# A convolution and gated MLP on one core: the steady step as one flat list, instruction by instruction

## The chip, the core and the metric

The kernel runs on one core of one Trainium2 chip. The metric is device time in microseconds for one execution. Before the change three executions gave 2262.18 to 2262.81 us, median 2262.51. Engine names are those of the profile: PE (TensorE matmul), PEld (its weight loads), DVE (VectorE), ACT (ScalarE), POOL (GpSimd), SP (SyncE, which here only issues DMAs).

## The reference

All data is fp32. `x` is 8 × 4096 × 192; a causal convolution of 7 taps with weights per head, then an MLP of width 2048 with the quick gelu:

```python
w = exp(weight - max(weight)); w = w / (sum(w) + 1e-9)          # (8 heads, 7 taps)
x_pad = concatenate([zeros(B, 6, D), x], axis=1)
c = einsum('hk,bskhg->bshg', w, x_pad[:, idx, :])               # causal, 7 taps, each head its weights
h = c.reshape(32768, 192) @ w_in                                # (192, 2048)
g = h * (1.0 / (1.0 + exp(-1.702 * h)))
out = g @ w_out                                                 # (2048, 192)
```

## The kernel before

The 32768 tokens go through in 32 steps (`big`), each 2 × 512 tokens, and every step has two matrix products. Both are done by bilinear forms in the manner of Strassen: some products of blocks are saved, at the price of sums of blocks before and after.

**First product** (`product1`, L598), `x` by `w_in`. A step has two halves (`v`) of 20 terms, listed in `TERMS`; each term is two calls, one per row group of the PE array (partitions 0 to 63 and 64 to 127, tiles of 64 × 128, 512 columns). That is 80 calls. They write PSUM tiles of two banks (`slots`, `sums`; a tile is a name like "a4" while it is in use), which are then combined: DVE sums (`sum2`, L639), ACT copies, also with changed sign (`copy2`, L633 and L635) and the gelus on ACT (`gelu`, L615 from PSUM, L620 from SBUF), which write the blocks of `g`. A call of an fp32 matmul is two weight loads and two passes in the profile.

**Second product** (`second`, L837; `one_matmul`, L855), `g` by `w_out`. It uses tiles of 128 × 32 and 256 columns, so four column strips of PE can run side by side: three main strips (the three chunks of one form) and one side strip, which works through other forms chunk by chunk. `go` (L871) issues three main calls and one side call, 78 times: 312 calls. When a chunk of the side strip is done, an ACT copy takes it to SBUF (L880), written directly behind that call. The main strips go to `mains = (bs[0], bx[0], by[0])`, the side strip to `sides = (bx[1], bs[1], by[1])`, the six banks of the three PSUM tiles that are free at that point. Around it stand DVE sums of blocks of `g` (`sum_g`, L355 and L357), accumulating transfers issued by POOL (`acc`, L831), seeds and joins of partial results (ACT L884, DVE), the 32 × 32 turns of the result on DVE (L771) and the stores on SP (L782).

**Convolution of later steps.** In between, the next steps' inputs are made: loads of `x` (`load_x`, L78, SP), transposes (L438, DVE), taps on ACT (`tap`, L483), their sums by POOL additions (`next_add`, L501) or accumulating transfers (`add_taps`, L506, POOL), sums of the blocks (`sums_c`, on POOL) and transfers to the other half of the partitions (`cross`, L526, SP).

**What sets the order.** The program has a manual schedule: each engine executes its instructions in the order in which they are written, and semaphores join the engines. The steady step is written by two lists, `ORDER` for the first product and `PLAN` for the second, and by queues of pending work beside them (`todo`, `ready`, `adds`, `tree`, `pieces`, `sums_left`): an entry like `("tap",)` or `("add", 4)` takes the next item or items of a queue, and `need`, `end_taps` and the loops at the end of `second` empty what is left. A term, a sum or a copy of `ORDER` is always written for both banks at once, and `("go", n)` always writes three main calls and one side call. The opening has a list of its own (`OPENING`).

Of the kernel before, what the change touches and what calls it, by code (L numbers as in the profile page):

```python
# [10 lines left out]
AF = mybir.ActivationFunctionType  # L11
# [4 lines left out]
def kernel(  # L16
# [149 lines left out]
    def side(big, other, b):  # L166
        return cross_of(big, b) if other else slot_of(big, b)
# [20 lines left out]
    def form(i):  # L188
# [8 lines left out]
    COPY_O = [  # L197
        [(10, 2), (16, 1), (17, 0), (18, 0), (8, 7), (9, 5), (11, 3, -1), (12, 6, -1)],
        [(13, 3), (14, 3), (15, 0), (19, 4), (20, 4), (21, 5), (22, 7)],
        [],  # L200
        [(23, 1), (24, 1), (1, 14), (7, 0, -1)],
    ]
    SUMS_O = [
# [4 lines left out]
    ]  # L208
    TURN_O = (9, 17, 20, 21)

# [105 lines left out]
    def split_rest(i, part=slice(0, PIECE)):  # L316

        lo, hi, m, e = words(i, part)
        ef = e.bitcast(F32)
        act.activation(ef, e, AF.Relu, bias=bias[:, 0:1], scale=-1.0)  # L320
        act.activation(e, ef, AF.Relu, bias=bias[:, 1:2], scale=-(2.0**23))
# [43 lines left out]
    w_left = list(SUMS_W)  # L365

    def next_w(n):
        for _ in range(n):
            add_up(lambda j: w_in_s[:, j, :], *w_left.pop(0))

# [6 lines left out]
    def round_o(i):  # L377
# [15 lines left out]
        round_piece(NW + i, dsts)  # L393

    def add_forms(stage):
        for dst, src, *sign in COPY_O[stage]:
            if sign:
                act.mul(form(dst), form(src), -1.0)
            else:
                act.copy(form(dst), form(src))  # L400
        for dst, src in SUMS_O[stage]:
            nc.gpsimd.dma_start(out=form(dst), in_=form(src), accum_op=ALU.add)

    def end_forms():
        for i in TURN_O:
            act.mul(form(i), form(i), -1.0)
# [45 lines left out]
    def tap_home(big, c, k):  # L452
        if big == 1:
# [8 lines left out]
    def conv(big, c, k, ns=slice(0, 2), times=vec.tensor_scalar_mul):  # L462
        src = conv_src(big, c, k, ns)
        dst = own(big)[:, 2 * c + ns.start : 2 * c + ns.stop, :]
        tap = cw[:, c, k : k + 1]
        if k == 0:
            times(dst, src, tap)
# [5 lines left out]
    DMA_TAPS = (0,)  # L473
    TAPS_IN = (0, 2, 1)
    ADDS_IN = [(1, 6), (2, 5), (2, 6)] + [(c, k) for c in (2, 1) for k in range(1, K) if (c, k) not in ((1, 6), (2, 5), (2, 6))]
    TREE = {2: [(1, 2)], 4: [(3, 4)], 6: [(5, 6), (0, 1), (3, 5), (0, 3)]}
    TREE_1 = {2: {2: [(1, 2)], 4: [(3, 4), (0, 1)], 6: [(5, 6), (0, 3), (0, 5)]}, 0: {2: [(1, 2)], 4: [(3, 4)], 6: [(5, 6)]}}

    def tap(big, c, k):

        dst = own(big)[:, 2 * c : 2 * c + 2, :]
        home = tap_home(big, c, k) if k else dst
        act.mul(home, conv_src(big, c, k), cw[:, c, k : k + 1])  # L483
        if k and c not in DMA_TAPS and big > 1:
            adds.append((ADDS_IN.index((c, k)), dst, home))
            adds.sort(key=lambda a: a[0])
            if big == 2:
                next_add()
            return
        homes = [dst] + [tap_home(big, c, i) for i in range(1, K)]  # L490
        for a, b in (TREE if big > 1 else TREE_1[c]).get(k, ()):
            tree.append((homes[a], homes[b]))
        if big < 3:
            end_taps(2 if big == 2 and k == K - 1 else 0)

    tree, adds = [], []

    def next_add():
        if adds:
            _, dst, home = adds.pop(0)  # L500
            nc.gpsimd.tensor_add(dst, dst, home)  # L501

    def add_taps():
        if tree:
            out, src = tree.pop(0)
            nc.gpsimd.dma_start(out=out, in_=src, accum_op=ALU.add)  # L506

    def add_pair(c, a, b):

        dst = own(1)[:, 2 * c : 2 * c + 2, :]  # L510
        homes = [dst] + [tap_home(1, c, i) for i in range(1, K)]
        vec.tensor_add(homes[a], homes[a], homes[b])

    def end_taps(left=0):
        while len(tree) > left:
            add_taps()
# [13 lines left out]
    def copy_over(b):  # L530

        for o in range(2):
            act.copy(conv_t[halves[1 - o], cross_of(0, b), :], own(0)[halves[o], b, :])

    pieces, sums_left = [], []
    LAST_AT = {s[0]: i for i, s in enumerate(SUMS_C)}
    ENDS = (NBLK, NBLK + 3, NBLK + 6, NB - 2, NB)
    GROUPS = [range(*ends) for ends in zip(ENDS, ENDS[1:])]  # L540

    def cross_piece():
        if pieces:
            cross(*pieces.pop(0))

    def cross_blocks(big):

        bs = list(REST)
        while bs:
            n = 1  # L550
            while n < min(3, len(bs)) and bs[n] == bs[0] + n:
                n += 1
            pieces.append((big, bs[0], bs[0] + n))
            bs = bs[n:]

    def next_sum():
        if sums_left:
            big, i = sums_left.pop(0)
            sums_c(big, *SUMS_C[i])
            for b in GROUPS:  # L560
                if max(LAST_AT[s] for s in b) == i:
                    pieces.append((big, b[0], b[-1] + 1))

    def begin_sums(big):
        sums_left.extend((big, i) for i in range(len(SUMS_C)))

    def prepare(big):

        for k in range(K if big < 3 else 0):
            yield "", 0.76 if k else 0.48, lambda k=k: conv(big, 1, k)  # L570
        yield f"conv {big}", 0.0, lambda: None
        def done():
            need(f"taps {big}")
            while adds:
                next_add()
            if OPEN_SUM:
                sums_c(big, *OPEN_SUM)
            cross(big, OPEN, OPEN + 1)

        yield f"done {big}", 0.0, done  # L580

    def prepare_taps(big):

        order = [(c, k) for c in (0, 2) for k in range(K)]
        if big > 2:
            order = [(c, 0) for c in TAPS_IN] + [(c, k) for c in TAPS_IN for k in range(1, K)]
        for c, k in order:
            yield "", 1.0, lambda c=c, k=k: tap(big, c, k)
        yield f"taps {big}", 0.0, lambda: None

    def product1(slot, a, b, big, v, first=False):
# [3 lines left out]
        for h in range(2):  # L595
# [11 lines left out]
    ALL = slice(0, TOK)  # L607

    def gelu(b, u, v, src, sign=1):
# [3 lines left out]
        if isinstance(src, list):  # L613
            for h in range(2):
                act.activation(  # L615
                    dst[:, :, h, :], src[h].rearrange("p (o t) -> p o t", o=2), AF.Gelu_apprx_sigmoid,
                    scale=float(sign),
                )
        else:
            act.activation(  # L620
                dst.rearrange("p o h t -> p h o t"),
                src.rearrange("p h (o t) -> p h o t", o=2),
                AF.Gelu_apprx_sigmoid,
                scale=float(sign),
            )
# [3 lines left out]

    def copy2(dst, src, sign=1):  # L630
        for h in range(2):
            if sign == 1:
                act.copy(bank(dst, h), bank(src, h))  # L633
            else:
                act.mul(bank(dst, h), bank(src, h), -1.0)  # L635

    def sum2(op, dst, a, b):
        for h in range(2):
            op(*(bank(t, h) for t in (dst, a, b)))  # L639

    def plain(u, m, n, v, slot, ks=range(NC), first=0):

        for k in ks:
            product1(slot, NC * (2 * u + m) + k, 2 * k + n, 0, v, k == first)

    ORDER = [
        (0, "prod", 6, "a8"), (0, "sum", "k0", "a8", "-", "k8"), (0, "prod", 2, "a3"), (0, "copy", "k4", "a3", 1),
        (0, "prod", 12, "a2"), ("tap",), ("tap",), ("tap",), ("tap",), ("add", 4), (0, "prod", 16, "a0"),
# [615 lines left out]
```

## Time and profile before

| what | us |
|---|---|
| median of three executions | 2262.51 |
| profiled execution: time | 2262.78 |
| profiled execution: span | 2261.1 |
| PE busy in the span | 2248.2 |
| DVE busy | 1985.3 |
| ACT busy | 1707.7 |
| POOL busy | 1063.9 |
| a steady step, first product and second | 35.42 and 33.95 |
| start of the second product of step 1 | 136.80 |

The page gives busy times over the whole span, the chain of work that ended last, and groups of instructions by line. PE's passes overlap, so it counts as busy while it waits for a fraction of a microsecond; where it waits is read from the starts of its weight loads and passes in the timeline. Row times are from the span's start. In a row of the timeline, the bracket gives the idle time before it and what ended it.

### The profile page before, as it was taken

The numbers are of one execution on the slowest core, as the hardware profiler recorded it, in microseconds if no ns is written. First come the engines' busy times: TensorE is split into PE (matmuls) and PEld (weight loads), VectorE is DVE, ScalarE is ACT, GpSimd is POOL, SyncE is SP. The second block draws the span as 40 slices with busy tenths as digits, with TensorE's granted clock in tenths as the row PEclk, the third lists the DMA queues.
The fourth block names the chain that finished last, engine by engine and source line by source line (L and its number), as shares of the span: only waits on it lengthen the run. The fifth ranks groups of instructions, "written<-read, shape, count | busy, mean of one in ns | idle before, by whom it ended". The sixth has DMA issues, their size and how long they took to land.

```text
span 2261.1 us, 62136 instructions
## 1 busy us (share of the span) xinstructions
PE 2248.2 (99%) x24966; PEld 1552.0 (69%) x24966; DVE 1985.3 (88%) x2970; ACT 1707.7 (76%) x3233; POOL 1063.9 (47%) x1098
## 2 busy tenths in 40 slices
PE   9999999999999999999999999999999999999999
PEld 5366567766777766777667776667776677766775
DVE  8998888988889888889888898888988888988888
ACT  8677877777777778777787777787777877777754
POOL 1545544455543555444555445554355544455510
PEclk9999999999999999999999999999999999999999
DMA  8986657766667666576565776666866657765543
GB/s 198 174 158 133 125 114 150 143 128 127 121 131 159 128 128 126 111 160 140 125 132 114 141 152 128 129 124 118 163 134 128 124 114 151 144 127 103 104 92 71
DMA packets 275679, 298.05 MB, mean 132 GB/s; under 512 B 119104, under 2 KB 203328, under 8 KB 275392
## 3 DMA queue, kind: packets, MB, share of 16 engines
q0 software_dynamic: 57648, 150.69, 37.0%
q1 hardware_dynamic: 216096, 142.99, 27.8%
q8 instruction: 198, 3.24, 0.6%
q14 instruction: 89, 0.73, 0.1%
q10 hardware_dynamic: 1648, 0.39, 0.1%
HBM read 53.15 MB, written 25.17 MB: 35 GB/s over the span
## 4 chain that ended last, share of the span: by engine, by line
PE 96%; DVE 2%; ACT 1%; issue 1%; DMA 1%; POOL 0%; DVEq 0%; ACTq 0%; POOLq 0%; SPq 0%
PE slot L598 49%; PE slot L855 45%; PE slot L1120 1%; DVE g L357 1%; DMA g<-osbs 0%; PE slot L1115 0%; DVE room L357 0%; ACT g L615 0%; PE slot L946 0%; DVE room L639 0%; ACT w_form L483 0%; DMA xin<-in_x_dram 0%; DVE slot L639 0%; DVE room L355 0%; DVE osbs L771 0%
## 5 line engine op out<-in xcount | busy, mean ns | idle before, releaser
L598 PE MATMUL slot<-conv_t,w_in_s 64*128 64x512 f32 x5152 | 1147.4, 594 | 3.3 <-ACT room L633 1.5
L598 PEld LDWEIGHTS slot<-conv_t,w_in_s 64*128 64x128 f32 x5152 | 663.3, 186 | 474.6 <-issue 312.1
L855 PE MATMUL slot<-g,w_form 128*32 128x256 f32 x9672 | 894.2, 379 | 0.7 <-DVE room L357 0.7
L855 PEld LDWEIGHTS slot<-g,w_form 128*32 128x32 f32 x9672 | 575.6, 110 | 128.9 <-DVE room L357 2.1
L501 POOL TENSOR_TENSOR conv_t<-conv_t,g 128x512 f32<-128x512 f32 x354 | 449.0, 1275 | 88.4 <-ACT g L483 65.4
L855 PE MATMUL slot<-g,w_out_s 128*32 128x256 f32 x5952 | 467.5, 379 | 1.3 <-DVE g L357 0.8
L357 DVE TENSOR_TENSOR g<-g 128x1024 f32<-128x1024 f32 x372 | 450.4, 1224 | 8.0 <-DMA g<-osbs 1.0
L880 ACT COPY room<-slot 32x256 f32<-32x256 f32 x651 | 237.2, 364 | 289.8 <-PE slot L855 281.5
L639 DVE TENSOR_TENSOR room<-slot,room 128x512 f32<-128x512 f32 x620 | 383.6, 679 | 67.8 <-PE slot L598 67.8
L633 ACT COPY room<-slot 128x512 f32<-128x512 f32 x620 | 337.7, 595 | 77.7 <-PE slot L598 61.7
L483 ACT ACTIVATE g<-xt,cw 128x512 f32<-128x512 f32 x534 | 353.9, 715 | 3.7
L620 ACT ACTIVATE g<-room 128x1024 f32<-128x1024 f32 x248 | 265.7, 1071 | 79.0 <-DVE room L639 49.3
L615 ACT ACTIVATE g<-slot 128x512 f32<-128x512 f32 x528 | 282.5, 610 | 51.9 <-PE slot L598 32.8
L831 POOL DMA_DIRECT2D g<-g x124 | 128.1, 1038 | 355.0 <-PE slot L855 330.8
L639 DVE TENSOR_TENSOR slot<-slot,room 128x512 f32<-128x512 f32 x372 | 239.7, 689 | 53.8 <-PE slot L598 52.2
L855 PEld LDWEIGHTS slot<-g,w_out_s 128*32 128x32 f32 x5952 | 239.7, 110 | 43.2 <-DVE room L639 23.3
L355 POOL TENSOR_TENSOR conv_t<-conv_t 128x256 f32<-128x256 f32 x210 | 179.3, 860 | 129.2 <-PE slot L598 119.6
L855 PE MATMUL slot<-osbs,w_form 128*32 128x256 f32 x2232 | 229.5, 379 | 0.0
L506 POOL DMA_DIRECT2D g<-g x120 | 105.9, 883 | 238.1 <-ACT g L483 99.4
L855 PEld LDWEIGHTS slot<-osbs,w_form 128*32 128x32 f32 x2232 | 132.5, 110 | 23.6
L639 DVE TENSOR_TENSOR slot<-room,slot 128x512 f32<-128x512 f32 x124 | 79.8, 687 | 41.8 <-PE slot L598 41.8
L855 PE MATMUL slot<-room,w_form 128*32 128x256 f32 x1488 | 112.9, 379 | 0.0
(166 smaller groups left out, 1662.6 us busy)
## 6 DMA issues: line engine op xcount, KB each, us to landing
g<-g POOLq DMA_DIRECT2D x124, 512.0 KB, 6.5
xin<-in_x_dram SPq DMA_DIRECT2D x240, 180.0 KB, 4.2
conv_t<-conv_t SPq DMA_DIRECT2D x186, 192.0 KB, 5.4
g<-g POOLq DMA_DIRECT2D x120, 256.0 KB, 5.4
conv_t<-conv_t SPq DMA_DIRECT2D x186, 128.0 KB, 2.9
out_dram<-osbs SPq DMA_DIRECT2D x186, 128.0 KB, 2.7
g<-room POOLq DMA_DIRECT2D x31, 512.0 KB, 5.1
conv_t<-g POOLq DMA_DIRECT2D x60, 256.0 KB, 5.4
```

Source lines behind the costliest of these rows:

```text
L355: eng.tensor_add(v(dst), v(a), v(b))
L357: eng.tensor_sub(v(dst), v(a), v(b))
L483: act.mul(home, conv_src(big, c, k), cw[:, c, k : k + 1])
L501: nc.gpsimd.tensor_add(dst, dst, home)
L598: nc.tensor.matmul(slot[h], w_in_s[halves[h], a, v * P : (v + 1) * P], src, start=first, stop=True, skip_group_check=True,)
L615: act.activation(dst[:, :, h, :], src[h].rearrange("p (o t) -> p o t", o=2), AF.Gelu_apprx_sigmoid, scale=float(sign),)
L620: act.activation(dst.rearrange("p o h t -> p h o t"), src.rearrange("p h (o t) -> p h o t", o=2), AF.Gelu_apprx_sigmoid, scale=float(sign),)
L633: act.copy(bank(dst, h), bank(src, h))
L639: op(*(bank(t, h) for t in (dst, a, b)))
L831: nc.gpsimd.dma_start(out=spot(dst), in_=spot(a), accum_op=ALU.add)
L855: nc.tensor.matmul(dst, w, t, start=first, stop=last, skip_group_check=True)
L880: act.copy(to, d)
```

## The change

`ORDER`, `PLAN` and the queues are gone. One flat list `STEP` has every instruction group of a steady step by itself, and `run(STEP, big)` writes it for steps 2 to 31; `OPENING` likewise has steps 0 and 1. The arithmetic of a step, its 80 and 312 matmul calls and its numbers of sums, copies, gelus and transfers stay. What differs in a steady step:

- Terms, sums, copies and gelus are written per bank (last argument 0 or 1), and the order of terms differs somewhat. Sums and copies of one bank may stand apart from those of the other.
- `("m", i)` is three main calls, `("s", i)` one side call, `("t", i)` the copy of a finished side chunk. Side and main calls are no longer one to one in order: the list begins with `s 0`, `m 0`, `s 4`, `s 5`, `m 2`, `s 2`.
- `sides` is now `(by[1], bx[1], bs[1])`; `mains` is unchanged.
- Of the POOL additions eleven stand in half 0 of the first product and one in half 1. One tap is left in the first product, the others are in the second.
- The loads of `x` come behind the transposes in half 0. Three of the crosses are in the first product, four in the second; all six accumulating transfers of the taps are in the second.

```diff
-    def product1(slot, a, b, big, v, first=False):
+    def product1(slot, a, b, big, v, first=False, hs=range(2)):
...
-        for h in range(2):
+        for h in hs:
...
-        mains, sides = (bs[0], bx[0], by[0]), (bx[1], bs[1], by[1])
+        mains, sides = (bs[0], bx[0], by[0]), (by[1], bx[1], bs[1])
...
+    STEP = [
+        ("prod", 0, 6, "a8", 1), ("prod", 0, 6, "a8", 0), ("sum", 0, "k0", "a8", "-", "k8", 0),
+        ("prod", 0, 12, "a2", 0), ("prod", 0, 2, "a3", 1), ("tap", 1, 1, 6), ("add", 1, 1, 6),
+        ("prod", 0, 12, "a2", 1), ("prod", 0, 2, "a3", 0), ("prod", 0, 16, "a0", 1), ("prod", 0, 16, "a0", 0),
+        ("sum", 0, "k0", "a8", "-", "k8", 1), ("copy", 0, "k4", "a3", 1, 1), ("sum", 0, "a1", "a2", "-", "k0", 0),
+        ("prod", 0, 9, "a2", 0), ("prod", 0, 15, "a3", 1), ("copy", 0, "k4", "a3", 1, 0),
...
+        ("sum", 0, "k5", "a1", "-", "k1", 0), ("prod", 0, 1, "a1", 1), ("sum", 0, "k5", "a1", "-", "k1", 1),
+        ("prod", 0, 10, "a4", 0), ("copy", 0, "a5", "a4", -1, 0), ("prod", 0, 18, "a2", 0), ("prod", 0, 18, "a2", 1),
+        ("add", 1, 1, 4), ("add", 1, 2, 6), ("add", 1, 2, 1), ("xt", 2, 0), ("xt", 2, 2), ("load", 3),
+        ("prod", 0, 10, "a4", 1), ("copy", 0, "a5", "a4", -1, 1), ("prod", 0, 17, "a1", 0), ("prod", 0, 17, "a1", 1),
+        ("copy", 0, "k6", "a2", 1, 1), ("copy", 0, "k6", "a2", 1, 0), ("prod", 0, 19, "a4", 0),
+        ("prod", 0, 19, "a4", 1), ("sum", 0, "a6", "k6", "-", "a4", 0), ("prod", 0, 11, "a1", 0),
+        ("gelu", 0, 0, 1, "a1", 1, 0), ("prod", 0, 11, "a1", 1), ("gelu", 0, 0, 1, "a1", 1, 1),
...
+        ("gelu", 1, 3, 1, "k3", 1, None), ("sum", 1, "k5", "a1", "-", "k1", 0), ("prod", 1, 11, "a1", 0),
+        ("copy", 1, "a5", "a4", -1, 0), ("prod", 1, 19, "a4", 0), ("copy", 1, "a5", "a4", -1, 1),
+        ("prod", 1, 19, "a4", 1), ("copy", 1, "k6", "a2", 1, 0), ("copy", 1, "k6", "a2", 1, 1),
...
+        ("prod", 1, 4, "a6", 1), ("gelu", 1, 0, 0, "a6", 1, 1), ("prod", 2, 0, "a3", 0),
+        ("sum", 1, "k7", "a7", "-", "k6", 1), ("prod", 1, 13, "a4", 1), ("prod", 1, 13, "a4", 0),
+        ("sum", 1, "k9", "a4", "-", "k0", 0), ("vsum", 1, 9), ("sum", 1, "k9", "a4", "-", "k0", 1),
+        ("gelu", 1, 0, 0, "a6", 1, 0), ("begin", 0), ("s", 0), ("final",), ("m", 0), ("s", 4), ("s", 5), ("m", 2),
+        ("s", 2), ("m", 1), ("m", 6), ("m", 5), ("s", 1), ("vsum", 1, 6), ("m", 7), ("m", 4),
+        ("gelu", 1, 2, 0, "k7", 1, None), ("gsum", 14, 14, "-", 18), ("s", 7), ("s", 8), ("m", 3),
...
+        ("tap", 2, 0, 4), ("tree", 2, 0, 3, 4), ("s", 46), ("t", 9), ("m", 50), ("gsum", 20, 20, "-", 11), ("s", 49),
...
+        ("join", "k2", "k2", "-", "k1"), ("turn", 1, 1, 1, "k2"), ("tree", 2, 0, 0, 1), ("turn", 1, 0, 0, "k6"),
+        ("m", 76), ("join", "k1", "p3", "-", "k3"), ("join", "k2", "p2", "-", "k4"), ("end",), ("store", 0, 0),
+        ("turn", 0, 0, 1, "k1"), ("turn", 0, 1, 1, "k2"), ("tree", 2, 0, 3, 5), ("s", 68), ("t", 18), ("m", 77),
+        ("m", 74), ("m", 75), ("join", "k1", "p5", "+", "k5"), ("tap", 2, 2, 6), ("store", 0, 1),
+        ("cross", 1, 12, 14), ("join", "k8", "k8", "+", "k0"), ("turn", 0, 1, 0, "k1"), ("tap", 2, 2, 4),
+        ("turn", 1, 1, 0, "k8"), ("store", 1, 0), ("store", 1, 1), ("tap", 2, 1, 1), ("tree", 2, 0, 0, 3),
     ]
...
+    def main_part(i):
+        dst, w, t, first, last = now["todo"][i]
+        for c in range(NC):
+            one_matmul(chunk(dst, c), w[:, chunk_cols(c)], t, first, last)
+
+    def side_part(i):
+        d, w, t, first, to = now["aside"][i]
+        one_matmul(d, w, t, first, to is not False)
...
+    opening()
+    for big in range(2, N_BIG):
+        run(STEP, big)
```

More of the change, by code (lines that the diff above doesn't have):

```diff
@@ L528, in cross, with copy_over @@
             )
[L530 to L589, printed above, removed]
-    def product1(slot, a, b, big, v, first=False):
+    def copy_over(b, o):
+        act.copy(conv_t[halves[1 - o], cross_of(0, b), :], own(0)[halves[o], b, :])
+    def product1(slot, a, b, big, v, first=False, hs=range(2)):
         s, c = slot_of(big, b), cross_of(big, b)
@@ L1211 @@
[L1211 to L1233 removed]
+            fcopy=form_copy,
```

694 lines of the change are left out of this document (275 added, 419 removed), and 282 rows, old and new, of tables (MAINS, OPENING, ORDER, PLAN).

## The prediction

> **What bounds the kernel now.** First the page: which engine is full, and whose work makes the chain.
>
> ```profile
> span 2261.1 us, 62136 instructions
> PE 2248.2 (99%) x24966; PEld 1552.0 (69%) x24966; DVE 1985.3 (88%) x2970; ACT 1707.7 (76%) x3233; POOL 1063.9 (47%) x1098
> PEclk9999999999999999999999999999999999999999
> PE 96%; DVE 2%; ACT 1%; issue 1%; DMA 1%; POOL 0%; DVEq 0%; ACTq 0%; POOLq 0%; SPq 0%
> ```
>
> PE is full at a full clock, and the chain that ends last is PE for 96%. The change leaves PE's calls as they are (80 and 312 in a step), so only PE's lost time can be won. Next the busy time by windows, one window to a product: two steady steps, then the second product of step 1 and the first of step 2.
>
> ```profile
> 1007.50:1042.92 35.42, 35.42 (x161) 20.68 (x160) 29.86 (x45) 28.71 (x50) 25.02 (x24) 1.00 0.54 112
> 1042.92:1076.87 33.95, 33.95 (x626) 28.69 (x625) 31.02 (x47) 24.82 (x52) 9.40 (x11) 1.00 0.79 154
> 1076.87:1112.28 35.41, 35.41 (x161) 20.67 (x161) 29.85 (x45) 28.68 (x50) 25.02 (x24) 1.00 0.54 113
> 1112.28:1146.22 33.94, 33.94 (x625) 28.81 (x624) 31.02 (x47) 24.80 (x52) 9.40 (x11) 1.00 0.77 152
> ...
> 136.80:172.90 36.10, 34.93 (x625) 22.97 (x625) 33.63 (x46) 24.92 (x52) 11.60 (x14) 1.00 0.79 154
> 172.90:209.09 36.19, 35.94 (x164) 21.98 (x160) 29.79 (x45) 28.71 (x50) 26.61 (x25) 1.00 0.56 119
> ```
>
> The columns are length, then PE, PEld, DVE, ACT, POOL, granted clock, DMA share, GB/s. A steady step is 35.42 + 33.95 = 69.37 us and repeats to 0.02. PE counts as busy throughout, because its passes are pipelined; the lost time shows only in the rhythm of the weight loads. They are in the timeline of the first product (start, length):
>
> ```profile
> 1010.19 0.19 PEld L598 LDWEIGHTS slot<-conv_t,w_in_s 64*128 64x128 f32 x2 [0.24 <-issue]
> 1010.78 6.89 PEld L598 LDWEIGHTS slot<-conv_t,w_in_s 64*128 64x128 f32 x33 [0.40 <-ACT room L633]
> 1017.91 0.52 PEld L598 LDWEIGHTS slot<-conv_t,w_in_s 64*128 64x128 f32 x3 [0.24 <-issue]
> 1018.82 0.29 PEld L598 LDWEIGHTS slot<-conv_t,w_in_s 64*128 64x128 f32 x2 [0.39 <-POOL conv_t L501]
> 1019.29 0.29 PEld L598 LDWEIGHTS slot<-conv_t,w_in_s 64*128 64x128 f32 x3 [0.18 <-ACT slot L635]
> 1019.78 0.23 PEld L598 LDWEIGHTS slot<-conv_t,w_in_s 64*128 64x128 f32 x2 [0.20 <-issue]
> ...
> 1024.08 0.23 PEld L598 LDWEIGHTS slot<-conv_t,w_in_s 64*128 64x128 f32 x2 [0.20 <-issue]
> ...
> 1035.23 0.34 PEld L598 LDWEIGHTS slot<-conv_t,w_in_s 64*128 64x128 f32 x2 [0.17 <-issue]
> 1035.73 0.19 PEld L598 LDWEIGHTS slot<-conv_t,w_in_s 64*128 64x128 f32 x1 [0.16 <-issue]
> 1036.12 0.29 PEld L598 LDWEIGHTS slot<-conv_t,w_in_s 64*128 64x128 f32 x2 [0.20 <-ACT slot L635]
> 1036.62 0.29 PEld L598 LDWEIGHTS slot<-conv_t,w_in_s 64*128 64x128 f32 x3 [0.21 <-ACT slot L635]
> 1037.09 0.26 PEld L598 LDWEIGHTS slot<-conv_t,w_in_s 64*128 64x128 f32 x2 [0.17 <-issue]
> ...
> 1041.87 0.29 PEld L598 LDWEIGHTS slot<-conv_t,w_in_s 64*128 64x128 f32 x2 [0.30 <-DVE slot L639]
> ```
>
> From 1019.78 to 1024.08 ten pairs of loads take 4.30 us: 0.43 us for a pass on each of the two row groups. A product has 160 passes, 80 a group: 34.4 us. So 35.42 holds 1.0 us of loss. Three waits are legible. At 1010.78 a pair comes 0.59 after the last, 0.16 late. From 1017.91 to 1019.78 eight loads (four pairs, 1.72) take 1.87: 0.15. From 1035.23 to 1037.09 again eight take 1.86: 0.14. The rest, 0.55, lies at the ends: the wait of 0.30 at 1041.87, and the turn to the other tile shape.
>
> The second product's rhythm, in PE's timeline:
>
> ```profile
> 1000.57 0.39 PE L855 MATMUL slot<-g,w_out_s 128*32 128x256 f32 x3
> 1000.72 0.38 PE L855 MATMUL slot<-g,w_form 128*32 128x256 f32 x1
> 1000.78 0.39 PE L855 MATMUL slot<-g,w_out_s 128*32 128x256 f32 x3
> ...
> 1007.04 0.39 PE L855 MATMUL slot<-g,w_out_s 128*32 128x256 f32 x3
> ...
> 1041.45 1.54 PE L598 MATMUL slot<-conv_t,w_in_s 64*128 64x512 f32 x4
> 1042.92 0.42 PE L855 MATMUL slot<-g,w_out_s 128*32 128x256 f32 x3
> 1043.11 0.38 PE L855 MATMUL slot<-g,w_form 128*32 128x256 f32 x1
> ```
>
> From 1000.57 to 1007.04 are 30 rounds, 0.2157 each, in which three main strips and the side strip make a pass apiece; 156 rounds are 33.65, so 33.95 loses only 0.3, and 0.19 of that is the side strip's later start (1043.11 against 1042.92).
>
> **The change part by part.** *The sign-changed copies.* "a5" is the copy of "a4" with changed sign (L635), and product 19 takes that PSUM place again. Before, the calls go 10, 17, 19, one of each per row group: between the end of 10 and the start of 19 lies one call, 2 × 0.43 = 0.86 us, for this copy:
>
> ```profile
> 1087.53 1.07 ACT L635 ACTIVATE slot<-slot 128x512 f32<-128x512 f32 x2 [0.25 <-PE slot L598]
> ```
>
> The pair takes 1.07, and PE's wait at 1019.29 and 1036.12 names it. The new list puts another call (18, or 11) between on one row group in each half of the step: 1.72 us for the copy; on the other group the copy can start without the first before it. Both late stretches should go: 0.15 + 0.14 = 0.29 us a step. Late next is the sum "a6" in half 0, where I see no row above 0.1; I charge nothing. The wait at 1010.78 is a copy "k4" that the call using its slot follows at the same distance in both lists: it stays.
>
> *The end of the first product.* Four passes take 1.54 where two per group side by side would be 0.86 and a last tail: one group trails, after the 0.30 us wait. The new list gives the last two calls (13) to the two groups in the other order, and the sums ahead of them (a7, k7) are split by bank. Between 0 and 0.30, I take half: 0.15 a step.
>
> *Start of the second product.* The list begins with a side call, then the main strips. An instruction that waits holds what is behind it, so the mains now start no earlier than the side: up to the 0.19 us above. The side's first bank moves from bx[1] to by[1], which the last sum of the first product frees. I take the whole 0.19, and put the bounds at 0 and one sum later:
>
> ```profile
> L639 DVE TENSOR_TENSOR room<-slot,room 128x512 f32<-128x512 f32 x620 | 383.6, 679 | 67.8 <-PE slot L598 67.8
> ```
>
> that is, 0.68 us.
>
> *Uneven strips.* Counted over the new list, the side strip is 4 calls ahead to 3 behind the mains, where before it went in step; 38 side calls stand directly behind another side call. Every strip still has 78 calls, so if PE can look past the waiting call this costs nothing. The rows at 1000.57 show that it looks past some: a call's two passes stand together in the program, yet the side's pass falls between the two of a main call, so at least four calls are in its view. I counted the rounds of calls that the new order needs: 78 with ten calls in view, 80 with seven, 95 with four. A round is 0.43, so between 0 and 17 × 0.43 = 7.3 us a step; the old order needs 78 with four and 104 with three, so at a view of four it would stand at its very edge, and its rows show 0.3 us of loss in all. I take 0.
>
> [...]
>
> *Adds, copies, sums.* Twelve adds on POOL now stand apart between the calls of the first product (eleven in half 0), three conv taps go from the first product to the second, nine conv sums stay in half 1. POOL's own pace is what decides:
>
> ```profile
> 1077.75 0.86 POOL L506 DMA_DIRECT2D conv_t<-g  x1 [2.98 <-DMA g<-g]
> 1081.27 15.90 POOL L501 TENSOR_TENSOR conv_t<-conv_t,g 128x512 f32<-128x512 f32 x12 [2.66 <-ACT g L483]
> ...
> L615 ACT ACTIVATE g<-slot 128x512 f32<-128x512 f32 x528 | 282.5, 610 | 51.9 <-PE slot L598 32.8
> ```
>
> Twelve adds take 15.90, 1.325 each. The step's last accumulating transfer is issued at 1077.75, 0.88 into the first product, and the adds begin at 4.40, so 2.66 us of slack cover the transfers. In the new list six of these (L506) stand at the second product's end, two pairs waiting for one another's landing. The adds come in another order too: the one of tap (2,6), third before, is seventh, and ends at 4.4 + 7 × 1.325 = 13.7. The gelu that overwrites its source stands behind call 29 of 80, which has drained at 29 × 0.43 and one pass, some 13.0; so it can now be 0.7 late. It takes 0.61 (L615) and is done at 14.3; the next fresh PSUM place is wanted by call 35, at 15.0. I charge 0, with 0.7 of cover left; if the adds begin that much later, each further 0.1 is lost 30 times.
>
> *Transfers.* The eight loads of x (L78) move from 1029.86 (22.4 into the product) to about 13, past the crosses on SP; three of the seven crosses are in the first product:
>
> ```profile
> 1028.65 1.11 SPq L526 DMA_DIRECT2D conv_t<-conv_t  x2
> 1029.86 4.04 SPq L78 DMA_DIRECT2D xin<-in_x_dram  x8
> 1034.01 6.76 SPq L526 DMA_DIRECT2D conv_t<-conv_t  x6
> ```
>
> Before, six crosses queue right behind the loads; in the new list the next one is some 20 calls later. The first product's DMA share is 0.54: no term.
>
> *Separate side copies* (L880) follow their call later; the strip goes on in another half bank meanwhile, so no term. *Opening*: step 1's second product has the side's new banks; it has waited 36.10 − 33.95 = 2.15 longer than a steady one. I take +0.5 there, −0.3 at the start of step 2 (0.77 above steady), so +0.2.
>
> **The sum.** 30 first products × −(0.29 + 0.15) = −13.2; 30 second × +0.19 = +5.7; opening +0.2: −7.3. The profiled execution took 2262.78 (span and 1.7 about it); 2255.5. The median of the three is 0.27 less, inside their range of 0.63, so I keep 2255.5 (−0.3%).
>
> **The rivals.** *A wash*: the 0.29 goes, the end's 0.15 does not, and the start costs 0.19 to 0.3: 30 × −0.1 to 0: 2259.5 to 2263. For it: DVE is 88% busy in both products, and a wait passed on is the usual fate. Against: the two L635 waits have no second claimant within 0.1 us.
> *More*: the first product comes to its rhythm, 34.4 + 0.4 at the ends, 0.6 gained, and the second loses nothing: 2262.78 − 18 = 2245. For it: every lost piece is a wait of PE. Against: the wait at 1010.78 stays.
> *Slower by the view of calls*: if seven calls are in view, two rounds more, 0.86 × 30 = +26 on the sum: 2281. It decides from a view of eight down (79 rounds, +13). For it: no row shows more than four. Against: the old order, at its edge with four, runs at 0.3 from its rhythm.
> *Slower by POOL's chain*: six transfers in a row at the end, at this landing:
>
> ```profile
> g<-g POOLq DMA_DIRECT2D x120, 256.0 KB, 5.4
> ```
>
> If the last is issued after about 4 us of the first product instead of 0.88 to 3, adds, gelus and calls shift alike; 10% on 5.4, on two that wait for one another, is 1.1 us, of which the cover takes 0.2: 0.9 × 30 = +27 on the sum, 2283. For it: the DMA share there is 0.79 already. Against: fewer other transfers are issued there.
> *Strict order*: if calls may not pass one another at all, each of the 38 side calls behind a side call costs a round of passes: 38 × 0.2157 × 30 = +246: 2501. [...]
>
> **How the numbers follow.** Forecast (2251 to 2258) 0.42; wash 0.20; more 0.10; view 0.11; POOL's chain 0.16; strict order 0.01. Measurement tells 0.2% (4.5 us) from no change. Faster: 0.42 + 0.10; same: the wash, 0.20; slower: 0.28. The range 2246 to 2283 leaves 0.2 out, half of each slower case above it.
>
> **What would show it.** Right: windows of about 35.0 and 34.1 in a step; PE's waits on "ACT slot L635" gone; one "ACT room" wait near 3.3 us left. Wrong: a second product above 34.5 with main strips idle beside a running side strip (view); the adds of POOL beginning later than 4.5 us into the first product, or ACT's gelus waiting for POOL (chain).

## The result: 5.7% slower, nearly all of it in the second product

The changed kernel takes 2391.99 us (2391.79 to 2393.76, four executions) against 2262.66 for the kernel before (four executions): a ratio of 1.0573, interval 1.0555 to 1.0592, or +129.3 us. The forecast was 2255.5, with a range of 2246 to 2283.

The page of the changed kernel: span, busy times, clock, chain.

```profile
span 2392.0 us, 61548 instructions
PE 2374.7 (99%) x24966; PEld 1478.0 (62%) x24966; DVE 2033.4 (85%) x2970; ACT 1710.3 (71%) x3233; POOL 1104.0 (46%) x1098
PEclk9999999999999999999999999999999999999999
PE 97%; DVE 1%; ACT 1%; issue 0%; DMA 0%; SPq 0%; DVEq 0%; ACTq 0%
L745 PE MATMUL slot<-g,w_form 128*32 128x256 f32 x9672 | 1019.6, 381 | 2.8 <-DVE room L345 1.9
```

The same number of passes, 381 ns for one where it was 379, the same clock: on this page PE is simply full, and no engine looks worse. (Only the group of 9672 passes hints at something: together they cover 1019.6 us, where before it was 894.2.) The windows say where the time is: a steady step, then the second product of step 1 and the first of step 2.

```profile
983.79:1019.34 35.55, 35.55 (x163) 22.76 (x160) 30.59 (x45) 28.70 (x50) 26.09 (x24) 1.00 0.54 112
1019.34:1057.45 38.11, 38.08 (x625) 23.59 (x624) 31.97 (x46) 24.90 (x52) 10.12 (x13) 1.00 0.69 134
...
136.77:173.39 36.62, 34.66 (x624) 23.65 (x625) 34.01 (x48) 25.66 (x54) 11.59 (x14) 1.00 0.79 154
173.39:208.95 35.56, 35.56 (x161) 22.72 (x161) 30.31 (x44) 28.38 (x48) 26.54 (x24) 1.00 0.58 120
```

The second product takes 38.11 instead of 33.95 (+4.16), the first 35.55 instead of 35.42 (+0.13): 30 × 4.29 = 129. PE's timeline of a second product shows the form of the loss:

```profile
1023.93 0.39 PE L745 MATMUL slot<-g,w_out_s 128*32 128x256 f32 x3
1023.98 0.59 PE L745 MATMUL slot<-g,w_form 128*32 128x256 f32 x2
1024.39 0.42 PE L745 MATMUL slot<-g,w_out_s 128*32 128x256 f32 x3
...
1025.92 0.59 PE L745 MATMUL slot<-g,w_form 128*32 128x256 f32 x2
1026.35 0.59 PE L745 MATMUL slot<-osbs,w_form 128*32 128x256 f32 x2
1026.78 0.38 PE L745 MATMUL slot<-g,w_form 128*32 128x256 f32 x1
1026.79 0.42 PE L745 MATMUL slot<-osbs,w_form 128*32 128x256 f32 x3
```

The main strips start at 1023.93 and next at 1024.39, 0.46 later instead of 0.22: of the two passes in the side strip's row at 1023.98 the first goes with the mains, the second runs alone. From 1025.92 the side strip runs four passes alone, until the mains start again at 1026.79. Counted from the starts of all 624 passes in the trace, this second product has 173 rounds instead of 156: in 17 of them only the side strip starts a pass, in 17 others only the mains. The 17 rounds more are 3.7 us. The waits of the weight loads do not explain that; in one whole second product and the start of the next first one they are

```profile
PEld slot L745 <- ACT g L500: 0.8, 1, 0.8
PEld slot L745 <- ACT room L781: 0.7, 2, 0.5
PEld slot L483 <- issue: 0.4, 1, 0.4
PEld slot L745 <- ACT room L537: 0.3, 1, 0.3
PEld slot L745 <- DVE room L345: 0.2, 1, 0.2
```

Together that is 2.4 us, against 1.2 in the same stretch of the kernel before (0.8 at the turn to the second product and 0.4 of issue).

### The profile page after: what moved, and what is told of

It is laid out like the page before. It is cut to its first block, busy times and chain, and to the rows that moved or that the text cites. A ratio compares the mean times of both kernels' runs of the same rounds, so it can differ in the third digit from the quotient of the medians.

```text
span 2392.0 us, 61548 instructions
## 1 busy us (share of the span) xinstructions
PE 2374.7 (99%) x24966; PEld 1478.0 (62%) x24966; DVE 2033.4 (85%) x2970; ACT 1710.3 (71%) x3233; POOL 1104.0 (46%) x1098
## 3 DMA queue, kind: packets, MB, share of 16 engines
q0 software_dynamic: 57648, 150.69, 34.9%
## 4 chain that ended last, share of the span: by engine, by line
PE 97%; DVE 1%; ACT 1%; issue 0%; DMA 0%; SPq 0%; DVEq 0%; ACTq 0%
PE slot L745 50%; PE slot L483 47%; DVE g L345 0%; DVE room L345 0%; ACT g L500 0%; DMA xin<-in_x_dram 0%; ACT w_form L446 0%; ACT conv_t L1120 0%; DVE xt L407 0%; ACT w_form L539 0%; DVE osbs L516 0%; DVE conv_t L441 0%; DVE slot L343 0%; DVE room L343 0%; ACT conv_t L446 0%
## 5 line engine op out<-in xcount | busy, mean ns | idle before, releaser
L745 PE MATMUL slot<-g,w_form 128*32 128x256 f32 x9672 | 1019.6, 381 | 2.8 <-DVE room L345 1.9
L483 PEld LDWEIGHTS slot<-conv_t,w_in_s 64*128 64x128 f32 x5152 | 725.5, 186 | 416.0 <-issue 151.2
L745 PEld LDWEIGHTS slot<-g,w_form 128*32 128x32 f32 x9672 | 517.8, 110 | 295.3 <-ACT g L500 24.3
L537 ACT COPY room<-slot 128x512 f32<-128x512 f32 x806 | 408.1, 540 | 252.5 <-PE slot L745 163.5
L745 PE MATMUL slot<-g,w_out_s 128*32 128x256 f32 (+1 forms) x6048 | 534.1, 385 | 1.7 <-DVE g L345 0.8
L343 POOL TENSOR_TENSOR conv_t<-conv_t 128x256 f32<-128x256 f32 x210 | 229.3, 1097 | 165.4 <-PE slot L483 158.0
L745 PE MATMUL slot<-osbs,w_form 128*32 128x256 f32 x2232 | 295.8, 383 | 0.0
L500 ACT ACTIVATE g<-room 128x1024 f32<-128x1024 f32 x248 | 264.5, 1066 | 21.1 <-DVE room L345 20.0
L343 DVE TENSOR_TENSOR room<-slot,room 128x512 f32<-128x512 f32 (+1 forms) x248 | 136.2, 550 | 76.6 <-PE slot L745 45.6
L345 DVE TENSOR_TENSOR slot<-slot,room 128x512 f32<-128x512 f32 x248 | 160.3, 692 | 31.7 <-ACT room L537 31.6
L343 DVE TENSOR_TENSOR slot<-slot,room 128x512 f32<-128x512 f32 (+1 forms) x155 | 93.3, 638 | 80.2 <-ACT room L537 40.9
```

What stands on the lines that cost most here:

```text
L343: eng.tensor_add(v(dst), v(a), v(b))
L345: eng.tensor_sub(v(dst), v(a), v(b))
L483: nc.tensor.matmul(slot[h], w_in_s[halves[h], a, v * P : (v + 1) * P], src, start=first, stop=True, skip_group_check=True,)
L500: act.activation(dst, src, AF.Gelu_apprx_sigmoid, scale=float(sign))
L537: act.copy(dst, src)
L745: nc.tensor.matmul(dst, w, t, start=first, stop=last, skip_group_check=True)
```

## The experiments

A time without an interval is that of a single execution.

The first theory was the prediction's rival of the view of calls, in the form that fits 4.2 us best: if only the first eight passes not yet started may start, in program order, the new list needs 177 rounds of passes instead of 156, 38.2 us by this count.

**The order measured by itself.** Behind the last step of the kernel before come blocks of calls of the second product's shape, in PSUM that is no longer used, with nothing to wait for.

```diff
         second(big, bx, bs, by, final, not more)
         free += [bx, by]
+    for size in (1, 2, 3, 4, 6):
+        for i in range(0, 48, size):
+            for kind in ["side"] * size + ["main"] * size:
+                w, t = form(0)[:, 0, :], spot(5)[:, 0, :]
+                if kind == "side":
+                    nc.tensor.matmul(slots[1][1][96:128, 0:T], w[:, 0:Q], t, start=True, stop=True, skip_group_check=True)
+                else:
+                    for c in range(NC):
+                        nc.tensor.matmul(
+                            slots[0][0][c * Q : (c + 1) * Q, 0:T], w[:, c * Q : (c + 1) * Q], t, start=True, stop=True,
+                            skip_group_check=True,
+                        )
```

> The kernel before, with five blocks of matmul calls behind its last step that nothing waits for: each block has 48 side calls and 48 times three main calls of the second product's shape, in groups of 1, 2, 3, 4 and 6 (so many side calls, then as many times three main calls). Their results are thrown away. Theory (PE can start a pass only if it is among the first eight that have not started, in program order): 96 rounds of 0.2157 us as a floor, so 20.7 us with groups of 1, 20.9 with 2, 21.1 with 3, 23.7 with 4, 28.3 with 6. Rival A (the uneven order costs nothing by itself, and the 4.2 us a step of the changed kernel come from waits for other engines): 20.7 to 20.9 in all five. Rival B (each side call directly behind a side call costs a round): 20.7, then 24 x 0.2157 = 5.2 more with 2, 32 rounds or 6.9 more with 3, 36 or 7.8 more with 4. Rival C (a view of ten or more passes): 20.9 with 3, 21.1 with 4.

The windows of the five blocks, groups of 1, 2, 3, 4 and 6:

```profile
2256.36:2277.08 20.72, 20.72 (x388) 12.48 (x384) 0.64 (x2) 0.00 (x0) 0.00 (x0) 1.00 0.13 26
2277.08:2297.82 20.74, 20.74 (x388) 12.53 (x384) 0.00 (x0) 0.00 (x0) 0.00 (x0) 1.00 0.01 2
2297.82:2318.54 20.72, 20.72 (x382) 13.93 (x378) 0.00 (x0) 0.00 (x0) 0.00 (x0) 1.00 0.01 2
2318.54:2339.71 21.17, 21.17 (x383) 13.57 (x376) 0.00 (x0) 0.00 (x0) 0.00 (x0) 1.00 0.01 2
2339.71:2368.11 28.40, 28.40 (x388) 16.61 (x380) 0.00 (x0) 0.00 (x0) 0.00 (x0) 1.00 0.01 2
```

Groups up to four cost at most 0.45 us (21.17 beside 20.72), groups of six 7.7. So order alone can cost time (against rival A), a side call behind a side call costs nothing as such (against B: 20.74 with groups of two), and C, which stood on 20.9 and 21.1 for three and four, fits these two rows, but with ten passes in view over all strips six would take 24.8, and less with more. The first theory failed too: 23.7 for four, measured 21.17. The timeline of the groups of six shows the loss (L1240 is the side call, L1243 the three main calls):

```profile
2341.44 0.38 PE L1240 MATMUL slot<-g,w_out_s 128*32 128x256 f32 x1
2341.47 1.47 PE L1243 MATMUL slot<-g,w_out_s 128*32 128x256 f32 x18
2342.57 0.40 PE L1240 MATMUL slot<-g,w_out_s 128*32 128x256 f32 x1
...
2343.24 1.46 PE L1240 MATMUL slot<-g,w_out_s 128*32 128x256 f32 x6
2344.32 0.42 PE L1243 MATMUL slot<-g,w_out_s 128*32 128x256 f32 x3
...
2344.99 1.47 PE L1243 MATMUL slot<-g,w_out_s 128*32 128x256 f32 x18
```

It repeats in 3.52 us (2341.47 to 2344.99) where 12 rounds are 2.59: the side strip starts at 2341.44 and next at 2342.57, 1.13 later, so of the six starts of the mains in the row at 2341.47 four are alone; the mains start at 2343.19 and next at 2344.32, also 1.13 later, and of the side's six passes from 2343.24 four start alone. No trace shows how PE holds its calls. What follows is the author's estimate, a count of rounds fitted to these starts and to the five block times: no strip has more than two calls begun or next in line (four passes), and the next call of a strip that has two keeps every call written behind it from starting, those of the other strips too. In groups of six each kind then starts nothing for four rounds, once in every group, as the rows have it. By this count the blocks need 20.7, 20.7, 21.1, 21.6 and 28.5 us; measured were 20.72, 20.74, 20.72, 21.17 and 28.40. The estimate became the theory; the expectations below call it "two calls ahead of time", which has to be read with the running call among the two, since the same count with three calls a strip gives 22.0 for the groups of six.

**The new list's order by itself.** The same, with a block of 78 alternating calls and a block in the order of the changed list (the edit is shown against the one above).

```diff
-    for size in (1, 2, 3, 4, 6):
...
+    for kinds in ("sm" * 78, mixed, ("s" * 5 + "m" * 5) * 15):
+        for kind in kinds:
...
```

`mixed` has a letter for each side or main call in the order of `STEP`.

> The kernel before, with two blocks of 78 side calls and 78 times three main calls behind its last step, whose results are thrown away and which nothing waits for: the first alternates, the second has the order of side and main calls of the changed kernel's steady step. Theory, formed after the groups were measured (each strip takes two calls, four passes, ahead of time; a third one holds all calls behind it): 33.65 us for the first and 170 rounds of passes, 36.7 us, for the second, so 3.0 of the changed kernel's 4.2 us a step are the order alone and 1.2 are waits for other engines. Rival A (one view of eight passes over all strips): 177 rounds, 38.2. Rival B (all of it waits): 33.7.

```profile
2256.11:2289.78 33.67, 33.67 (x628) 20.28 (x624) 0.76 (x2) 0.00 (x0) 0.00 (x0) 1.00 0.09 18
2289.78:2326.38 36.60, 36.60 (x620) 23.58 (x613) 0.00 (x0) 0.00 (x0) 0.00 (x0) 1.00 0.01 2
2326.38:2366.70 40.32, 40.32 (x602) 24.32 (x597) 0.00 (x0) 0.00 (x0) 0.00 (x0) 1.00 0.01 2
```

36.60, near the 36.7 of the estimate of two calls a strip, not 38.2 or 33.7. (The third block, groups of five 15 times, needs 39.7 by the same estimate; 40.32 were measured.) So 2.9 of the 4.16 us are the order alone, with no other engine involved. The estimate has 14 rounds in which the side runs alone and 14 of the mains alone, and the passes of this block start in just so many of each. One view over all strips of nine passes instead of eight, a rival that was not put up, gives 36.7 here as well. It fails on the groups of six (26.5 against 28.40), and by its count only two of the four strips would start in nine of the rounds here; in the trace none does, only all four, the three mains, or the side.

**Alternating again.** In the changed kernel only the interleaving of side and main calls is put back to one and three; each keeps the new order among its own kind.

```diff
-        ("gelu", 1, 0, 0, "a6", 1, 0), ("begin", 0), ("s", 0), ("final",), ("m", 0), ("s", 4), ("s", 5), ("m", 2),
-        ("s", 2), ("m", 1), ("m", 6), ("m", 5), ("s", 1), ("vsum", 1, 6), ("m", 7), ("m", 4),
+        ("gelu", 1, 0, 0, "a6", 1, 0), ("begin", 0), ("s", 0), ("final",), ("m", 0), ("s", 4), ("m", 2), ("s", 5),
+        ("m", 1), ("s", 2), ("m", 6), ("s", 1), ("m", 5), ("vsum", 1, 6), ("s", 7), ("m", 7),
...
```

> The changed kernel with the calls of the second product alternating again, one side call and then three main calls; the order among the side calls and among the main calls is the new one, all other instructions keep their order among themselves, and PSUM places are the new ones. Theory (view of eight passes): the 21 rounds of passes lost in a step come back, the second product falls from 38.12 to about 33.9 and the kernel from 2392 to 2392 - 30 x 4.2 = 2266 if the first product stays at 35.55; if its late sums were only a consequence of the uneven strips, it comes to about 35.1 and the kernel to 2253. Rival (new PSUM places, or the transfers and POOL): the second product stays above 37 and the kernel above 2370.

2293.9 us, a ratio of 1.0138 (1.0121 to 1.0155) to the kernel before. Its windows:

```profile
312.99:349.10 36.11, 35.81 (x165) 23.24 (x161) 30.64 (x45) 29.26 (x51) 25.72 (x23) 1.00 0.55 114
349.10:383.41 34.31, 34.15 (x625) 19.92 (x624) 31.80 (x46) 24.31 (x51) 10.03 (x12) 1.00 0.76 149
```

The second product comes back by 3.8 us, to 34.31. The first product does not get better, as one half of the expectation had it, but worse, to 36.11, and the kernel stays 28 us above the 2266 expected: the first product starts behind a second product that is now shorter, and what it waits for was late anyway (below). Of the second product's 34.31, 0.36 above the kernel before are left; it has 156 rounds again, and two of them start late.

**Smaller drifts.** The changed kernel's order, with the side strip held to at most two, or at most three, calls ahead or behind. Where the order stays within that, it is the new one; the first places that differ:

```diff
-        ("seed", "p4", "p2", 1), ("m", 8), ("m", 10), ("s", 6), ("s", 9), ("m", 9), ("s", 3), ("seed", "k1", "p3", 1),
+        ("seed", "p4", "p2", 1), ("m", 8), ("s", 6), ("m", 10), ("s", 9), ("m", 9), ("s", 3), ("seed", "k1", "p3", 1),
...
```

```diff
-        ("s", 31), ("m", 15), ("gsum", 7, 8, "-", 7), ("s", 15), ("s", 26), ("s", 13), ("gsum", 8, 8, "-", 16),
+        ("s", 31), ("m", 15), ("gsum", 7, 8, "-", 7), ("s", 15), ("s", 26), ("m", 13), ("gsum", 8, 8, "-", 16),
...
```

> The changed kernel, in whose second product the side strip may be at most two calls ahead of or behind the main strips (from 4 ahead to 3 behind before this edit); 25 side calls still stand directly behind a side call, instead of 38. Theory (two calls of a strip ahead of time): no rounds lost, so the second product is as in the alternating order, 34.3, or up to 0.3 above; kernel 2290 to 2305. Rival A (one view of eight passes): 8 rounds of passes, 1.7 us a step above that, 36.0, kernel 2345. Rival B (each side call behind a side call costs a round): 25 rounds, 39.7.

> The same with at most three calls ahead or behind; 36 side calls directly behind a side call. Theory (two calls of a strip ahead of time): 10 rounds of passes lost, 2.2 us a step above the alternating order, 36.5 and with its waits up to 37.3; kernel 2360 to 2380. Rival A (one view of eight passes): 20 rounds, 4.3 us, 38.6.

```profile
351.04:386.10 35.06, 34.96 (x626) 22.26 (x625) 31.78 (x46) 24.32 (x51) 10.05 (x12) 1.00 0.75 145
...
355.44:392.69 37.25, 37.22 (x625) 23.24 (x624) 31.88 (x46) 24.89 (x52) 10.88 (x13) 1.00 0.70 137
```

(first row: two; second row: three.) 2318.0 and 2371.8 us. Three calls fall within the theory's 36.5 to 37.3. Two calls take 35.06, which is 0.75 above the alternating order where 0 to 0.3 was expected (2318.0 where 2290 to 2305 was), though below the 36.0 of one view of eight passes. In the traces two calls have 158 rounds and three have 169, the estimate counts 156 and 166; with the 173 of the changed kernel against 170, each of these three uneven orders in a whole kernel has two or three rounds more than the estimate gives it. The order by itself (above) has none more, which leaves waits for other engines; which waits, no run separates.

**PSUM places alone**, in both directions: the old banks in the changed kernel, the new ones in the kernel before.

```diff
-        mains, sides = (bs[0], bx[0], by[0]), (by[1], bx[1], bs[1])
+        mains, sides = (bs[0], bx[0], by[0]), (bx[1], bs[1], by[1])
```

> The changed kernel with the side strip's banks as before, (bx[1], bs[1], by[1]), and nothing else. Theory (view of eight passes): the order of the calls is the same, so the second product stays at 38 or above and the kernel at 2390 or above; first product within 0.3 of 35.55. Rival (the new places cost the time): second product near 34, kernel near 2265.

> The kernel before with the side strip's banks of the change, (by[1], bx[1], bs[1]), and nothing else. Theory: no cost but a later start of the side strip, 0 to 0.19 us a step: 2262 to 2268. Rival (the new places cost the time): up to 4.2 us a step, 2390.

2422.0 us and 2264.7 (ratio 1.0010, 1.0000 to 1.0019). The places are not the cause; the new order is even 30 us worse without its own places: 35.93 and 38.84 in a step, with the same 173 rounds, and the first product is 0.38 from 35.55 where at most 0.3 was expected. In the kernel before they do this:

```profile
382.85:418.47 35.62, 35.62 (x164) 26.01 (x160) 30.44 (x45) 29.39 (x50) 25.27 (x25) 1.00 0.53 114
418.47:452.28 33.81, 33.81 (x626) 20.19 (x625) 31.02 (x46) 24.78 (x52) 9.40 (x11) 1.00 0.77 150
```

0.2 more in the first product, 0.14 less in the second.

**The sign-changed copy alone.** In the kernel before, the term 11 is put ahead of the term 19, in both halves, which gives the copy "a5" two calls instead of one.

```diff
-        (0, "copy", "a5", "a4", -1), (0, "copy", "k6", "a2", 1), (0, "prod", 19, "a4"), (0, "prod", 11, "a1"),
+        (0, "copy", "a5", "a4", -1), (0, "copy", "k6", "a2", 1), (0, "prod", 11, "a1"), (0, "prod", 19, "a4"),
...
-        (1, "prod", 19, "a4"), (1, "prod", 11, "a1"), ("vsum",), (1, "prod", 8, "a5"),
+        (1, "prod", 11, "a1"), (1, "prod", 19, "a4"), ("vsum",), (1, "prod", 8, "a5"),
```

> The kernel before with one edit in its list of the first product, in both halves: the term 11 goes ahead of the term 19, so that two calls instead of one lie between the end of 10 and the start of 19 on each row group, for the sign-changed copy a5. The prediction's first term alone: 0.29 us less in each first product, 2262.8 - 30 x 0.29 = 2254. Rival (the wait is passed on: the sum a6, which needs 19, now has one call less before term 5 takes its place): 2260 to 2265.

2268.5 us, a ratio of 1.0027 (1.0016 to 1.0038): slower, past the rival's own 2265. The waits of one first product, before and with the edit (totals, times, longest):

```profile
PEld slot L598 <- DVE slot L639: 0.8, 4, 0.3
PEld slot L598 <- ACT slot L635: 0.6, 3, 0.2
```

```profile
PEld slot L598 <- DVE slot L639: 2.2, 8, 0.5
```

The wait for the copy (L635) is gone, and the wait for DVE's sums grows by 1.4: "a6" needs term 19, which now comes later, and term 5, which takes the place of 19, has to wait for it.

**What holds the first product.** The weight loads of the first product in the changed kernel, where a pair should follow in 0.43:

```profile
986.47 0.19 PEld L483 LDWEIGHTS slot<-conv_t,w_in_s 64*128 64x128 f32 x2 [0.23 <-issue]
987.21 0.44 PEld L483 LDWEIGHTS slot<-conv_t,w_in_s 64*128 64x128 f32 x4 [0.54 <-DVE slot L345]
...
1017.69 0.29 PEld L483 LDWEIGHTS slot<-conv_t,w_in_s 64*128 64x128 f32 x2 [0.60 <-DVE slot L343]
1018.29 0.29 PEld L483 LDWEIGHTS slot<-conv_t,w_in_s 64*128 64x128 f32 x2 [0.30 <-DVE slot L343]
```

Two waits on DVE, one for the sum "a1" at the start, one for the sums "a7" at the end. The rows of DVE and of ACT ahead of them, and the same sum at the same place in the kernel before:

```profile
1014.79 2.24 DVE L345 TENSOR_TENSOR osbs<-osbs,g 128x1024 f32<-128x1024 f32 x1
1016.95 1.28 DVE L343 TENSOR_TENSOR slot<-slot,room 128x512 f32<-128x512 f32 x2
```

```profile
983.88 0.35 ACT L781 COPY room<-slot 32x256 f32<-32x256 f32 x1
984.13 2.56 ACT L446 ACTIVATE g<-xt,cw 128x512 f32<-128x512 f32 x4
986.72 2.05 ACT L537 COPY room<-slot 128x512 f32<-128x512 f32 x4
```

```profile
1038.92 1.69 DVE L357 TENSOR_TENSOR osbs<-osbs,g 128x1024 f32<-128x1024 f32 x1
```

A sum of 128 × 1024 takes 2.24 us here and 1.69 before, where most such sums take 1.22. In both kernels POOL's additions run beside it (1.60 us from 1016.02 here, 1.60 from 1039.60 before); why it takes 0.55 longer here, no run separates. And four taps stand on ACT between the last side copy and the copies of the first product. In the alternating kernel the start is the worse one:

```profile
316.99 0.44 PEld L483 LDWEIGHTS slot<-conv_t,w_in_s 64*128 64x128 f32 x4 [1.13 <-DVE slot L345]
```

Both suspects were taken out of it by leaving out work (so these kernels compute less than the reference): the sum, the last four taps, both. Only the entries taken out are shown:

```diff
-        ("gsum", 1, 1, "-", 11),
...
-        ("tap", 2, 1, 5), ("tap", 2, 2, 6), ("tap", 2, 2, 4), ("tap", 2, 1, 1),
```

> The kernel of the alternating order (second product 34.3, first 36.1), without one sum of the first product: the DVE sum of 128 x 1024 that stands ahead of the last term's sums (gsum 1, 1, -, 11). It leaves out a part of the computation, so only its time counts. Theory (the end of the first product is set by DVE, which runs that sum for 2.24 us beside POOL's additions): the wait of 0.59 at the end goes, first product about 35.5, kernel about 2275. Rival (PE's own order of calls costs the time): first product above 36.0, kernel above 2290.

> The kernel of the alternating order without the last four taps on ACT in each step (2,1,5 and 2,2,6 and 2,2,4 and 2,1,1), which stand around the last side copies; also a computation left out, only its time counts. Theory (the start of the first product is late because ACT is behind with taps, so that the last side copy, DVE's last joins and the copies k4 come late): the wait of 1.1 on DVE's sum a1 falls below 0.4, first product 35.1 to 35.4, kernel about 2268. Rival: the start is bound by DVE alone, first product above 35.9.

> The kernel of the alternating order without that sum and without those four taps (a computation left out). Theory (both waits are separate): first product 34.7 to 34.9, kernel about 2252. Rival (the one takes the other's place): no better than the better of the two alone.

2276.4, 2279.0 and 2260.6 us, where about 2275, 2268 and 2252 were expected. The first products, one row of each kernel's windows:

```profile
311.67:347.15 35.48, 35.19 (x165) 23.15 (x161) 28.59 (x44) 28.90 (x51) 24.86 (x23) 1.00 0.54 112
```

```profile
313.00:348.56 35.56, 35.56 (x165) 22.62 (x161) 30.61 (x45) 26.80 (x47) 25.81 (x23) 1.00 0.56 116
```

```profile
311.79:346.73 34.94, 34.94 (x164) 22.53 (x160) 28.55 (x44) 26.46 (x47) 24.93 (x23) 1.00 0.55 114
```

36.11 falls by 0.63, 0.55 and 1.17: the two add up, so they are separate waits. In the second the longest wait on a DVE sum fell from 1.1 to 0.6, not below 0.4, and the product to 35.56, not 35.4; with both left out it is 34.94, at the edge of the 34.7 to 34.9 expected. **One tap moved** from ahead of the last side copy to behind it, without leaving anything out (shown against the alternating kernel):

```diff
-        ("s", 72), ("t", 19), ("tap", 2, 1, 5), ("m", 76), ("s", 66), ("join", "k2", "k2", "-", "k1"),
+        ("s", 72), ("t", 19), ("m", 76), ("s", 66), ("join", "k2", "k2", "-", "k1"), ("turn", 1, 1, 1, "k2"),
...
-        ("t", 18), ("m", 75), ("join", "k1", "p5", "+", "k5"), ("tap", 2, 2, 6), ("store", 0, 1),
+        ("tree", 2, 0, 3, 5), ("s", 69), ("m", 74), ("s", 68), ("t", 18), ("tap", 2, 1, 5), ("m", 75),
```

> The kernel of the alternating order, in which one tap on ACT (2,1,5) is moved from ahead of the last side copy to behind it; nothing is left out. Theory (that copy is what DVE's last joins wait for): DVE's join no longer waits 0.48, the first product falls by 0.3 to 0.5 to 35.7, kernel about 2282. Rival (the copies k4 behind the taps decide): no change, 2294.

2294.1 us: no change, as the rival had it; so it is not the one side copy. That it is the amount of taps ahead of the copies "k4" fits both runs, but no run moves these taps behind the copies. None of the versions that compute everything beats the kernel before.

## Why the prediction was wrong, step by step

*Uneven strips* is the step that failed. "Between 0 and 7.3 us a step … I take 0": it costs 2.9 alone (36.60 against 33.67), and together with the waits for other engines the second product lost 4.16 (17 rounds more, 3.7 us, and the rest in rounds that start late). The bounds of this term held, the choice in them did not, and the range of the whole did not carry them: 7.3 us 30 times are 219, but it ended 27 above the sum. Two things were wrong in the choice. The limit was taken to be one view over all calls; the runs fit the estimate of two calls a strip better (21.6 and 36.7 for the measured 21.17 in groups of four and 36.60, where one view of eight passes gives 23.7 and 38.2). And the argument "at a view of four the old order would stand at its very edge, and its rows show 0.3 us of loss" proves nothing against a small limit: the old order alternates, and by the same way of counting it needs 156 rounds with three, four or five passes a strip, so its rhythm cannot tell them apart. The rival "view of calls" had the sign that came (main strips idle beside a running side strip, in 17 rounds of the second product), priced at seven calls; the same count gives 88 rounds, +4.3 us a step, with five in view, and that would have been near the measured 4.16 by luck: a view of five calls gives 23.7 for the groups of four, which took 21.17.

*Strict order* (0.01) did not come: with a round lost for every side call behind a side call, the 36 of them in 48 pairs in groups of four would add 7.8 us to the 20.72 alternating. The groups of four run in 21.17, so there passes of different strips overtook one another by several calls.

*The sign-changed copies* were right as a wait and wrong as a gain: "ACT slot" waits went from 18.1 us to 0.5 in the whole run, but the first product got 0.13 longer, not 0.29 shorter. The waits shown above for DVE's "a1" at the start and "a7" at the end stand in the changed kernel instead. "Late next is the sum a6 … I charge nothing" is not shown to be wrong there: term 5 is no nearer to term 19 in the new list. In the kernel before, where putting term 11 ahead brings 19 nearer to 5, the widening costs 6 us.

*The end of the first product*, −0.15: 0.60 and 0.30 of wait stand there instead of 0.30. DVE's sum of 2.24 us sets that end; without it the product falls by 0.63 (in the alternating kernel). Whose call comes first on which row group, which the term was about, no run separates.

*Start of the second product*, +0.19, does not show in the changed kernel: the wait of the weight loads at the turn is 0.8 us in both kernels. There the side's load ends a wait of 0.76 at 1019.34, the mains' loads follow at 1019.35, and the passes of both start at 1019.35. In the kernel before, the new places alone gave −0.14 in the second product and +0.20 in the first.

*POOL's chain and the transfers* were rightly charged nothing: DMA landings are shorter than before (3.5 us instead of 5.4 for the 256 KB transfers), and POOL appears among PE's waits nowhere in a steady step. POOL's additions begin 3.0 us into the first product that starts at 983.79 (at 986.78), where later than 4.5 was the sign of this rival.

```profile
g<-g POOLq DMA_DIRECT2D x120, 256.0 KB, 3.5
```

*Opening*: +0.52 for the second product of step 1 (+0.5 forecast), −0.63 for the first of step 2 (−0.3 forecast).

## What to carry to other kernels

For fp32 calls like these, on column strips that run side by side, interleave the strips' calls evenly in the program. Here a drift of up to three calls cost 2.9 us a step above the alternating order and up to two 0.75 (37.25 and 35.06 against 34.31), while regular groups of four cost 0.45 in 20.72 and groups of six 7.7. This shows neither as idle PE (99% busy in both kernels) nor in full as a wait (2.4 us instead of 1.2, for a loss of 4.16), but in the starts of the passes. A limit that the present order never reaches has no price in its trace: measure it with a block of calls behind the kernel before an order rests on it. And a wait that is removed from a chain in which DVE is 88% busy should be credited only after the next sum has been timed.

## What the runs showed of the hardware

All of this is for fp32 calls on four strips of 128 × 32 with 256 columns, three main strips and one side strip. Four strips started a pass each in 0.2157 us (30 rounds in a row, kernel before). 48 side calls with 48 times three main calls took 20.72 us alternating, 20.74 in groups of two, 20.72 in groups of three, 21.17 in groups of four and 28.40 in groups of six; in the groups of six the mains and the side in turn started nothing for some four rounds, with no other engine at work. 78 with 78 took 33.67 alternating and 36.60 in the order of the changed kernel.

The estimate of two calls a strip, fitted to the five times in groups and to the starts of the passes, gives 20.7, 20.7, 21.1, 21.6 and 28.5 for the groups, and 33.65 and 36.7 for the two orders. With three or five passes a strip instead of four the same count gives 31.7 or 25.2 for the groups of six. It is a way of counting rounds in these runs; no trace shows what in PE sets the limit.
